# Loads by three units in rows of 24 KB, stores by pairs or units from pair buffers, and two pairs in spent buffers

## Chip, cores, metric

One core of one Trainium2 chip. The metric is the device time of one execution in microseconds (us). Most executions of a kernel agree within a few tenths of a per cent; an execution more than 1.5% above the fastest of the same kernel counts as slow, and comparisons use fast executions only.

## The reference

Attention through 32 inducing points, then a feed-forward network without a residual. B = 4 batches, N = 12480 tokens, C = 128 channels, m = 32, hidden width 2048; everything enters and leaves in fp32.

```python
def mab(q, kv):
    s = scale * (q @ kv.transpose(0, 2, 1))
    s = s - s.max(-1, keepdims=True)
    a = np.exp(s)
    a /= a.sum(-1, keepdims=True) + 1e-09
    return a @ kv
h = mab(I, x)            # 32 inducing points attend to all tokens of a batch
y = mab(x, h)            # every token attends to the 32 rows of h
out = gelu(y @ w_in) @ w_out
```

## The kernel before

A batch is six units of 2048 tokens and a tail of 192. The *first pass* goes over the units of a batch as they are loaded: transposes on the tensor engine (PE), an evacuation into `xT`, scores against the inducing points, exponentials, and a gather into `hun`. When the tail is through, a short *chain* of matmuls makes `h` and `q`, the network applied to the 32 rows (the kernel does that on `h`, not on the tokens). The *second pass* makes scores from `xT`, exponentials, the products with `q`, scales them by the row sums on the vector engine (DVE), the scalar engine (ACT) or ACT and GpSimd (POOL), and stores them. The second pass of a batch runs beside the first pass of later ones.

What the change touches is how tokens are grouped for the DMA. Loads go by *pairs* of units: a partition's row of a pair is 32 tokens, 16 KB of fp32, cast to fp16 on the way, issued by GpSimd. Stores go by pairs from three pair buffers, issued by the sync engine (SP). Pair (b, p) is pair p of batch b. Pair (1, 2) is put into a buffer of `xT` that is no longer needed ("spent"). Batch 3 is stored unit by unit, in 8 KB rows, from six load buffers that have come free.

```python
XBUFS = 6
OBUFS = 3
...
APART = 3
SPENT = (B - 3, 2)
...
        self.pair = idx // 2
        self.c_pair = 0 if self.tail else 16 * (idx % 2)
        self.first = self.c_pair == 0
        self.last = self.tail or not self.first
        self.held = self.nc if self.tail else 32

    def rows_of(self, t):
        t0 = self.b * N + self.pair * 2 * SGT
        t = t[t0 : t0 + self.held * self.p, :]
        return t.rearrange("(p c) d -> p c d", p=self.p)
...
    def x_tile(u):
        if u.tail:
            xh = sb.tile([TP, 2, 128], FP16, tag="xht", bufs=3)
        else:
            xh = sb.tile([128, 32, 128], FP16, tag="xh", bufs=XBUFS)
...
    def a_load(u):
        nc.gpsimd.dma_start(out=x_tile(u), in_=u.rows_of(x_rows))
...
    def b_inverse(bt, u):          # where a unit's output lives
        ...
        elif u.b >= APART:
            o = sb.tile([128, 32, 128], FP16, tag="xh", bufs=XBUFS)
            ...
        else:
            if u.first:
                if spent(u):
                    pair = xt_pool.tile([128, N], FP16, tag="xT", name=f"spent{u.b}")
                    ...
                else:
                    pair = sb.tile([128, 32, 128], FP32, tag="o", bufs=OBUFS)
                bt.live[("pair", u.pair)] = pair
            o = bt.live[("pair", u.pair)][:, u.c_pair : u.c_pair + 16, :]
        bt.live[("o", u.idx)] = o
...
    def b_store(bt, u, alone):     # alone: a tail, or a unit of batch 3
        if alone:
            c0, c1, o = u.c_pair, u.c_pair + u.nc, bt.live[("o", u.idx)]
        else:
            c0, c1, o = 0, u.held, bt.live[("pair", u.pair)]
        nc.sync.dma_start(out=u.rows_of(out)[:, c0:c1, :], in_=o)
```

The order of instructions on each engine is fixed while the kernel is built: a list scheduler runs through all pieces with modelled durations, and a model of the DMA decides when a load or a store is done. That model gives each of the two queues half of the DMA while both have work:

```python
class Moves:
    ...
            steps += [h[1] * len(going) for h in going.values()]
    ...
                    h[1] -= step / len(going)
```

An engine that reaches a piece whose buffer is not yet free waits there, with all the work behind it in the fixed order.

## Time and profile before

| | before |
|---|---|
| device time, median (range) | 133.07 us (132.63 to 133.23, 5 runs) |
| profiled span | 131.5 us |
| DMA engines full | 3 to 128 us |
| compute ends | 121.1 us |
| stores of pair (0, 1) landed | 66.6 us |
| first DVE write into that buffer's next use | 68.22 us |
| first store of batch 3 issued | 108.6 us (one unit) |

### The profile page before, as it was taken

Reading aid. Unit: us, or ns where it says so; the run is one execution under the profiler, and the core shown is the slowest. Engines: PE = TensorE matmul, PEld = TensorE weight load, DVE = VectorE, ACT = ScalarE, POOL = GpSimd, SP = SyncE. Lnnn points to the kernel's source line nnn. Section 1 sums busy time; section 2 is a strip of 40 time slices with the busy share of each in tenths; the row PEclk is TensorE's granted clock in tenths of the full one; section 3 lists DMA queues with packets and bytes.
Section 4 is the critical chain, followed back from the end, with each engine's and each line's share of the span. In section 5 each row is a group of like instructions: output and inputs, shape, how many; then the busy total and the mean of one; then the engine's idle time right before and its main releaser. Section 6 shows DMA issues by size and latency. Waiting matters only on the chain. (4 is left out here: it accounts for less than half of the span.)

```text
span 131.5 us, 3505 instructions
## 1 busy us (share of the span) xinstructions
PE 101.8 (77%) x1365; PEld 60.0 (46%) x1365; DVE 91.9 (70%) x265; ACT 77.1 (59%) x177; POOL 65.6 (50%) x85
## 2 busy tenths in 40 slices
PE   0967789479999999999697699999999499781000
PEld 0255656278646557565362565735645312320000
DVE  1825447525899998999999367999899756997000
ACT  3006154426776879499787378889797457754000
POOL 7910131039634556894815367965269763483000
PEclk9999869855999999999999689999999856999555
DMA  5999999999999999999999999999999999999981
GB/s 152 298 228 209 217 198 219 218 214 222 214 209 214 214 229 339 306 387 368 322 304 339 277 251 297 316 401 411 439 425 415 419 444 419 411 426 424 431 349 43
DMA packets 5666, 40.17 MB, mean 305 GB/s; under 512 B 624, under 2 KB 1936, under 8 KB 2192
## 3 DMA queue, kind: packets, MB, share of 16 engines
q0 software_dynamic: 2848, 13.30, 49.9%
q1 hardware_dynamic: 2752, 26.61, 48.5%
q8 instruction: 11, 0.18, 0.5%
q10 hardware_dynamic: 48, 0.02, 0.1%
q14 instruction: 7, 0.06, 0.1%
HBM read 27.67 MB, written 25.56 MB: 405 GB/s over the span
## 5 line engine op out<-in xcount | busy, mean ns | idle before, releaser
L702 POOL TENSOR_TENSOR pair<-pair,rr 128x512 f32<-128x512 f32 x26 | 26.8, 1043 | 19.6 <-ACT pair L365 16.7
L686 PE MATMUL at<-q,e 128*128 128x512 f16 (+1 forms) x104 | 33.7, 391 | 3.6 <-DVE xT L363 1.2
L377 PE MATMUL tr<-identity_h,xh 128*128 128x128 f16 x392 | 32.7, 244 | 3.1 <-DMA xh<-in_x_dram 3.1
L377 PEld LDWEIGHTS <-xh 128*128 128x128 f16 x392 | 27.5, 111 | 9.2 <-DMA xh<-in_x_dram 4.2
L363 DVE COPY xT<-tr 128x1024 f16<-128x1024 f16 (+1 forms) x36 | 22.7, 646 | 10.1 <-PE tr L377 9.6
L365 ACT ACTIVATE xT<-tr 128x1024 f16<-128x1024 f16 (+1 forms) x16 | 15.7, 980 | 18.6 <-PE tr L377 18.5
L717 DVE TENSOR_TENSOR pair<-at,rr 128x512 f32<-128x512 f32 x36 | 23.3, 676 | 1.1 <-PE at L686 0.4
L287 POOL DMA_DIRECT2D xh<-in_x_dram x15 | 8.3, 555 | 21.3 <-DMA xh<-in_x_dram 10.5
L403 ACT ACTIVATE e<-s 128x512 f16<-128x512 f32 (+1 forms) x28 | 15.3, 546 | 5.7 <-PE s L391 5.4
L638 ACT ACTIVATE e<-s 128x512 f16<-128x512 f32 (+1 forms) x28 | 14.9, 562 | 3.4 <-PE s L626 1.8
L365 ACT ACTIVATE pair<-at 128x512 f32<-128x512 f32 x26 | 15.7, 602 | 1.1 <-PE at L686 1.0
L417 DVE STREAM_TRANSPOSE e1t<-e 128x256 int32<-128x256 int32 (+1 forms) x28 | 11.1, 399 | 3.4 <-ACT e L403 3.3
L686 PEld LDWEIGHTS <-e 128*128 128x128 f16 (+1 forms) x104 | 8.7, 103 | 10.2 <-issue 6.7
L425 PE MATMUL hun<-xh,e1t 128*32 128x128 f16 x392 | 10.8, 226 | 3.1 <-DVE e1t L417 3.0
L572 POOL TENSOR_TENSOR pt<-pt 128x512 f32<-128x512 f32 (+4 forms) x20 | 12.0, 602 | 2.1 <-DVE rr L661 0.7
L717 DVE TENSOR_TENSOR o<-at,rr 128x512 f32<-128x512 f32 (+1 forms) x19 | 10.5, 579 | 2.9 <-PE at L686 2.5
L391 PE MATMUL s<-xT,indT 128*32 128x512 f16 (+1 forms) x108 | 10.5, 379 | 1.4 <-DVE xT L363 0.8
L425 PEld LDWEIGHTS <-e1t 128*32 128x32 f16 x392 | 6.4, 98 | 8.9 <-DVE e1t L417 6.5
L626 PE MATMUL s<-xT,hT 128*32 128x512 f16 (+1 forms) x100 | 10.0, 407 | 0.5 <-DVE rr L661 0.5
L702 POOL TENSOR_TENSOR o<-o,rr 128x512 f32<-128x512 f32 x7 | 7.3, 1041 | 5.7 <-ACT o L365 3.3
L650 PEld LDWEIGHTS <-e 128*128 128x128 f16 (+1 forms) x104 | 5.7, 99 | 4.8 <-issue 1.9
L650 PE MATMUL r<-strand,e 128*128 128x4 f16 (+1 forms) x104 | 6.7, 168 | 0.2 <-ACT e L403 0.2
(76 smaller groups left out, 102.0 us busy)
## 6 DMA issues: line engine op xcount, KB each, us to landing
out_dram<-pair SPq DMA_DIRECT2D x8, 2048.0 KB, 15.0
xh<-in_x_dram POOLq DMA_DIRECT2D x11, 1024.0 KB, 28.2
out_dram<-o SPq DMA_DIRECT2D x6, 1024.0 KB, 8.8
out_dram<-spent SPq DMA_DIRECT2D x1, 2048.0 KB, 16.1
x_first<-in_x_dram SPq DMA_DIRECT2D x1, 1024.0 KB, 5.2
xh<-in_x_dram POOLq DMA_DIRECT2D x1, 512.0 KB, 6.9
w_in_h<-in_moe_w_in_dram POOLq DMA_DIRECT2D x1, 512.0 KB, 17.2
w_out_h<-in_moe_w_out_dram POOLq DMA_DIRECT2D x1, 512.0 KB, 19.2
```

The source lines that it names most:

```text
L363: nc.vector.tensor_copy(out=out, in_=in_)
L365: nc.scalar.activation(out=out, in_=in_, func=AF.Copy)
L377: nc.tensor.transpose(tr[:, c - c0, : u.p], xh[: u.p, c, :], identity_h[: u.p, : u.p])
L403: nc.scalar.activation(out=e1[: u.p, : u.nc // 2, :, :], in_=s1[: u.p, : u.nc, :].rearrange("r (a b) i -> r a i b", b=2), func=AF.Exp, sca ...
L417: nc.vector.transpose(out=pairs(e1t)[: u.p, :n], in_=pairs(e1)[: u.p, :n])
L425: nc.tensor.matmul(bt.hun[32 * j : 32 * j + 32, :], e1t[: u.p, c // 2, :, c % 2], xh[: u.p, c, :], start=u.idx == 0 and c < 4, stop=c + 4 ...
L572: nc.gpsimd.tensor_tensor(out=bt.pt[:, :, :, :half], in0=bt.pt[:, :, :, :half], in1=bt.pt[:, :, :, half : 2 * half], op=ALU.add,)
L638: nc.scalar.activation(out=e2[: u.rows, : u.cols], in_=s2[: u.rows, : u.cols], func=AF.Exp, scale=SCALE,)
L650: nc.tensor.matmul(r2[: u.p, ci, : u.nj], e2[: u.rows, ci * u.p : (ci + 1) * u.p], strand[: u.rows, : u.nj], start=True, stop=True,)
L686: nc.tensor.matmul(at[: u.p, : u.nj, :], e2[: u.rows, ci * u.p : (ci + 1) * u.p], bt.q[: u.rows, : u.nj, :], start=True, stop=True,)
L702: nc.gpsimd.tensor_tensor(out=part, in0=part, in1=rr2[: u.p, ci, : u.nj].unsqueeze(2).broadcast_to([u.p, u.nj, 128]), op=ALU.mult,)
L717: nc.vector.tensor_tensor(out=ov[: u.p, ci, :, :], in0=at[: u.p, : u.nj, :], in1=rr2[: u.p, ci, : u.nj].unsqueeze(2).broadcast_to([u.p, u. ...
```

## The change

The intent: longer rows for loads (24 KB, three units at once, called a *triple* below, so fewer packets and transfers), output by pairs also in batch 3, and no load buffers kept back for outputs. A pair that straddles two triples (pair 1 of each batch) cannot be one row of the new layout, so it is stored as two units in 8 KB rows.

```diff
-XBUFS = 6
+XBUFS = 4
-APART = 3
-SPENT = (B - 3, 2)
+SPENT = ((B - 3, 2), (B - 1, 0))
...
+        self.three = idx // 3
+        self.c_three = 0 if self.tail else 16 * (idx % 3)
+        self.leads = self.c_three == 0
+        self.held = self.nc if self.tail else 48
...
+        self.split = self.pair == 1
...
-        t0 = self.b * N + self.pair * 2 * SGT
+        t0 = self.b * N + self.three * 3 * SGT
...
-            xh = sb.tile([128, 32, 128], FP16, tag="xh", bufs=XBUFS)
+            xh = sb.tile([128, 48, 128], FP16, tag="xh", bufs=XBUFS)
...
-        elif u.b >= APART:
-            o = sb.tile([128, 32, 128], FP16, tag="xh", bufs=XBUFS)
...
+        c1 = u.c_three + u.nc
         if alone:
-            c0, c1, o = u.c_pair, u.c_pair + u.nc, bt.live[("o", u.idx)]
+            c0, o = u.c_three, bt.live[("o", u.idx)]
         else:
-            c0, c1, o = 0, u.held, bt.live[("pair", u.pair)]
+            c0, o = u.c_three - u.nc, bt.live[("pair", u.pair)]
...
-        elif u.first:
+        elif u.leads:
...
-                    move=part(u, LOAD_US) * (1 if u.tail else 2),
+                    move=part(u, LOAD_US) * (1 if u.tail else 3),
...
-        alone = u.tail or u.b >= APART
+        alone = u.tail or u.split
```

More of the change, by code (lines that the diff above doesn't have):

```diff
@@ L96, in __init__ @@
         self.last = self.tail or not self.first
-        self.held = self.nc if self.tail else 32
+        self.split = self.pair == 1
     def rows_of(self, t):
-        t0 = self.b * N + self.pair * 2 * SGT
+        t0 = self.b * N + self.three * 3 * SGT
         t = t[t0 : t0 + self.held * self.p, :]
@@ L106, in spent @@
 def spent(u):
-    return (u.b, u.pair) == SPENT
+    return (u.b, u.pair) in SPENT
 def home_of(u):
@@ L277, in x_tile @@
         else:
-            xh = sb.tile([128, 32, 128], FP16, tag="xh", bufs=XBUFS)
-        x_tiles[(u.b, u.pair)] = xh
+            xh = sb.tile([128, 48, 128], FP16, tag="xh", bufs=XBUFS)
+        x_tiles[(u.b, u.three)] = xh
         return xh
     def x_of(u):
-        xh = x_tiles[(u.b, u.pair)]
-        return xh[:, u.c_pair : u.c_pair + u.nc, :]
+        xh = x_tiles[(u.b, u.three)]
+        return xh[:, u.c_three : u.c_three + u.nc, :]
     def a_load(u):
@@ L292 @@
     x_first = sb.tile([128, 32, 128], FP32, tag="o", bufs=OBUFS)
-    x_pair = x_tile(units[0][0])
+    x_lead = x_tile(units[0][0])
     src = units[0][0].rows_of(x_rows)
     nc.sync.dma_start(out=x_first[:, :16, :], in_=src[:, :16, :])
-    nc.gpsimd.dma_start(out=x_pair[:, 16:, :], in_=src[:, 16:, :])
-    a_load(units[0][2])
+    nc.gpsimd.dma_start(out=x_lead[:, 16:, :], in_=src[:, 16:, :])
+    a_load(units[0][3])
     identity = consts.tile([128, 128], FP32)
@@ L367, in a_cast @@
     def a_cast(c0, engine):
-        evacuate(engine, x_pair[:, c0 : c0 + 8, :], x_first[:, c0 : c0 + 8, :])
+        evacuate(engine, x_lead[:, c0 : c0 + 8, :], x_first[:, c0 : c0 + 8, :])
     def halves(u):
@@ L665, in b_inverse @@
             o = sb.tile([TP, 2, 128], FP32, tag="ot", bufs=2)
-        elif u.b >= APART:
-            o = sb.tile([128, 32, 128], FP16, tag="xh", bufs=XBUFS)
-            o = o.rearrange("p c d -> p (c d)").bitcast(FP32)
-            o = o.rearrange("p (c d) -> p c d", d=128)
         else:
@@ L785, in add_load @@
                 plan.add(
-                    (0, 1), {"POOL": 0.55}, lambda e: None, takes=["xh"], move=LOAD_US
+                    (0, 1), {"POOL": 0.55}, lambda e: None, takes=["xh"], move=2 * LOAD_US
                 )
             )
-        elif u.first:
+        elif u.leads:
             loads.append(
@@ L793, in add_load @@
                     {"POOL": 0.55},
-                    lambda e: None if u.b == 0 and u.idx == 2 else a_load(u),
+                    lambda e: None if u.b == 0 and u.idx == 3 else a_load(u),
                     takes=["xht" if u.tail else "xh"],
-                    move=part(u, LOAD_US) * (1 if u.tail else 2),
+                    move=part(u, LOAD_US) * (1 if u.tail else 3),
                 )
@@ L876 @@
             takes=["hun"] if u.idx == 0 else [],
-            gives=["e1t"] + (["xht"] if u.tail else ["xh"] if u.last else []),
+            gives=["e1t"] + (["xht"] if u.tail else ["xh"] if u.idx % 3 == 2 else []),
         )
@@ L907 @@
         )
-        alone = u.tail or u.b >= APART
-        if alone:
-            o_taken = o_given = ["ot" if u.tail else "xh"]
+        alone = u.tail or u.split
+        if u.tail:
+            o_taken = o_given = ["ot"]
         else:
```

## The prediction

> **What bounds the kernel now.** I read the page's slices first, then the DMA part, the chain that ended last, the DMA issues with their landing times, and the DVE timeline around one store. From the page: the DVE row, the DMA row, the queues, and the last chain by engine.
>
> ```profile
> DVE  1825447525899998999999367999899756997000
> DMA  5999999999999999999999999999999999999981
> ...
> q0 software_dynamic: 2848, 13.30, 49.9%
> q1 hardware_dynamic: 2752, 26.61, 48.5%
> ...
> DVE 3%; PE 1%; issue 1%; ACT 0%
> ```
>
> The 16 DMA engines are full from slice 2 to slice 39 (3 to 128 us): the two queues together take 98% of their time. The compute engines stop at 121 us (last three slices of DVE empty), and the followed chain covers only 5% of the span: what ends at 131.5 us is the stores. So DMA work is the floor. But DVE at 9 tenths from 35 to 70 us and from 80 to 99 us says that compute is the next limit, close behind.
>
> Bytes: 27.67 MB read and 25.56 MB written, 405 GB/s over the span. With loads alone the queue writes 217 GB/s of halves, so reads about 430 GB/s; with stores alone it moves 425 to 430 GB/s. Both are nearly the same rate per byte.
>
> How the two queues share comes from two windows, 51 to 55 us (a load of a pair beside a store of a pair) and 76 to 80 us (the same load beside the 96 KB tail store of batch 0).
>
> ```profile
> q1 hardware_dynamic: 54, 0.88, 52.6%
> q0 software_dynamic: 50, 0.41, 48.8%
> ...
> q0 software_dynamic: 100, 0.69, 82.2%
> q1 hardware_dynamic: 106, 0.40, 26.1%
> ```
>
> Columns: queue, packets, MB, share of the engines' time in the window. In the first, rows are 16 KB on both sides and the packets are 54 to 50: one for one, each 0.62 us (52.6% of 64 us over 54). In the second, the packets are again about one for one, although most store packets there are 1 KB: the loads took 82% of the time. The tail's 6 packets per engine needed 4.0 us (previous store landed at 76.3, tail at 80.3), that is 6 x (0.62 + 0.05). So the queues alternate packet by packet, whatever the size. Packet size is therefore a priority.
>
> **What the Trainium skill says.** "DMA: Bandwidth & Descriptors", section "Queues, rings and completion order": each DMA engine round-robins between queue rows at packet granularity. The two windows agree. Its section "Where 436 GB/s comes from" puts the ceiling at 435 GB/s; the 425 to 430 GB/s here are 98 to 99% of it, so longer rows can win at most 1 to 2%. Its section "Bandwidth" has rates up to 425 GB/s for large loads, as here.
>
> **The change, part by part.**
> *Rows.* Eleven pair loads in 16 KB rows become one such load and seven in 24 KB rows. An 8 KB store row takes 0.31 us and a 16 KB row 0.62 us: no visible fixed cost per row. From 430 against 435 GB/s I estimate under 10 ns per row, so 512 rows fewer save about 512 x 10 ns / 16 = 0.3 us. Splitting one pair per batch into two unit stores, while batch 3 goes from six unit stores to two pairs and two units, adds 128 rows net, less than 0.1 us. Sum: nil, at best 0.3 us faster.
> *Engines.* The order of instructions moves four evacuations of the transposed input from ACT to DVE (4 x 0.65 us more) and four scalings off DVE (4 x 0.65 us less), leaving DVE's sum unchanged near 92 us. PE is unchanged; ACT changes by about 1 us.
> *Start.* Batch 0's units 1 and 2 come together, then 3 to 5. The last lands at 17 us as now, but three units wait for it instead of two. One unit costs PE some 2 us there at half clock, so I put the first store 1.5 to 2 us later, first packet at 49.5 instead of 48.1 us. This is hidden: loads fill the DMA then.
> *Sharing.* With 24 KB load rows (0.92 us, estimate from 0.62) against a pair's 16 KB rows, loads get 60%; against a unit's 8 KB rows, 75%. The split pair is pair 1 of each batch. In batch 0 its stores run just while batch 3's two triples load. Working with 8 rows per engine and transfer: the second triple of batch 2 lands near 56 us; the store of pair (0,0) near 58.6 (now 59.2); a small tail load to 59.5, in which 2.4 rows of the split pair pass; the other 13.6 rows each stand beside a load row: 13.6 x (0.92 + 0.31) = 16.7 us. So both stores of pair (0,1) have landed near 76 us. Now they land at
>
> ```profile
> out_dram<-pair SPq DMA_DIRECT2D x1, 2048.0 KB, 15.5
> ...
> 68.22 1.29 DVE L717 TENSOR_TENSOR pair<-at,rr 128x512 f32<-128x512 f32 x2
> ```
>
> issued 51.05 + 15.5 = 66.6 us. The second line, from DVE's timeline, is the first DVE write into that buffer by pair (1,1): 68.22 us, only 1.6 us after. Three pair buffers stay in the ring, so the changed kernel has the same reuse; its DVE, ACT and GpSimd orders all wait for both (0,1) stores at that place. In exchange batch 3's loads land earlier: about 69 and 79.5 us instead of 73.4 and 89.1.
>
> *What the stall costs.* At that instruction DVE has done 48 of its 95 us in both orders (instruction counts times mean durations of the page's groups). Batch 2's chain and all of batch 3's work stand behind it in DVE's fixed order. DVE would arrive at 69 to 70.5 us and wait until 77: 6 to 8 us. Of this, 2.2 us come back, since DVE now waits that long at 73 to 75 us for a PE that waits for batch 3's load; other waits recover little, because DVE's remaining 46.5 us plus the 4 us of waits around batch 3's chain end at 77 + 50.5 = 127.5. So compute ends at 126 to 128 instead of 121 us.
>
> *From compute to the end.* Now stores run 8 us behind compute, and at 98.5 us the backlog falls to 1.8 units (14 units issued, 12.2 stored), 4.4 us. Delays up to about 4 us are therefore hidden. Beyond, the DMA runs dry. Batch 3's first store is now a unit at 108.6 us; after the change a pair, whose second unit ends now at 111.8 us, so 117 to 118.5 us with the delay. The stores before it (18 units, 3 tails) are through by about 114. Restart at 118.5 to 119.5, then 6 units x 2.45 us = 14.7 us, the tail 0.3 and landing about 1 us: span 134.5 to 135.5, +3 to +4 us, times 136 to 137 from 133.07.
>
> **The rivals.**
> *Nothing changes: the floor holds.* The DMA carries the same bytes and the delay may be smaller than the backlog. For it: the 4.4 us slack, earlier batch 3 loads, a schedule arranged for late loads (batch 2's second pass runs further ahead). Then 132.5 to 133.5. Also so if a 24 KB row goes as two packets: loads then get about 60% against unit rows, the split pair lands near 71 us, and the stall is some 2 us.
> *Loads bound at the start and the larger grain costs.* Three units arriving at once could move all of batch 0 later by 3 us or more. Against it: the DMA is busy with loads up to 48 us anyway, and the next triples have free buffers. Adds 0 to 1 us.
> *Row length lifts the rate.* Against it: 98 to 99% of the ceiling already. Best case 131.5 to 132.5, not a gain of 2% (130.4).
> *Losing batch 3's separate output buffers.* Its six units now have six freed load buffers; after it, a spent buffer and the ring. Pair (3,1) waits for store (2,0), landing now at 104.6, and (3,2) for (2,1), at 109.6; the units need them after 111 us. Adds nothing.
>
> **Range and chances.** I hold the priority theory with its stall at about three in four, centred at 136.3 with 1.3 to either side; it leaves some cases under 2% (135.7). The rest is around 133. Between them: 135.6, range 132.6 to 138.6. Faster by 2% 0.04; within 2% 0.47; slower 0.49.
>
> **What would show it.** Right: in the changed profile, load packets of 0.92 us alternate one for one with store packets while both run; the unit stores of pair (0,1) land near 76 us; DVE, ACT and GpSimd wait at pair (1,1) for a DMA for 6 us or so; DVE ends near 127; the DMA row shows a hole near 110 to 119 us. Wrong: packets not longer than 0.62 us on the load queue; no DVE wait near 70 us; a DMA row full up to 128 us with a time near 133. A time under 131 would contradict the ceiling argument.

## The result, and the profile after

The changed kernel took 141.33 us (median of 5, 140.15 to 143.93; four of them fast) against 133.07 (132.63 to 133.23). The ratio is 1.0617, with a 95% interval of 1.0545 to 1.0689. Every ratio here is the mean time of one kernel's fast runs over the mean of the kernel before's fast runs of the same rounds (in the experiments without the profiled execution), so it is not quite the ratio of the medians quoted. The result is slower, as the prediction leaned, but above its range (132.6 to 138.6).

The page of the changed kernel, slices of 3.5 us and queues:

```profile
DVE  1732568213789898889900569989988745899200
PEclk9995599955699999999997579999999655896555
DMA  6999999999999999999999999999899790399991
...
q0 software_dynamic: 2272, 13.30, 46.7%
q1 hardware_dynamic: 2896, 26.61, 46.4%
```

The bytes are the same (13.30 MB of halves written by loads, 26.61 MB moved by stores and the first load), in 431 packets fewer, and the queues' packets together take 93.1% of 139.4 us, 130 us: the work of the DMA has not grown. What is new is two holes: DVE at 0, 0 and 5 tenths from 70 to 80 us, and the DMA at 0 and 3 tenths from 115 to 122 us. In the kernel before, the DMA row is full from the second slice to the 38th.

The first hole. How the two queues share from 68 to 72 us, where loads of batch 3 meet the unit stores of pair (0, 1) in the changed kernel and a pair store in the one before (queue, packets, MB, share of the engines' time). After:

```profile
q0 software_dynamic: 59, 0.60, 71.0%
q1 hardware_dynamic: 58, 0.48, 29.0%
```

Before:

```profile
q1 hardware_dynamic: 60, 0.98, 58.2%
q0 software_dynamic: 60, 0.39, 46.0%
```

Packets alternate one for one in both. Once the 24 KB rows stand against 8 KB rows (part of this window), loads take nearly three quarters. A 24 KB row takes 926 ns, an 8 KB row 309, a 16 KB row 611 to 625. The second unit store of pair (0, 1), from the list of issues between 52 and 53 us, with its size and the time to landing, then DVE's timeline where that buffer is used next:

```profile
out_dram<-pair SPq DMA_DIRECT2D x1, 1024.0 KB, 25.1
```

```profile
69.78 0.17 DVE L620 TENSOR_REDUCE sums<-pt 128x1 f32<-128x16 f32 x1
77.62 0.69 DVE L718 TENSOR_TENSOR pair<-at,rr 128x512 f32<-128x512 f32 x1 [7.67 <-DMA out_dram<-pair]
```

It was issued at 52.38 us and landed at 77.5, and DVE stood 7.67 us waiting for it. ACT waits 7.7 us for the same store, GpSimd 9.9 us behind ACT.

The second hole. SP's timeline of store issues after, then one stretch of it: window, length, busy us of PE, weight loads, DVE, ACT and POOL (with counts), granted clock (the part of its full clock that PE was given), share of the DMA, GB/s:

```profile
109.26 0.33 SPq L731 DMA_DIRECT2D out_dram<-pair  x1
109.69 0.37 SPq L731 DMA_DIRECT2D out_dram<-o  x1
120.40 0.33 SPq L731 DMA_DIRECT2D out_dram<-spent  x1
122.75 6.58 SPq L731 DMA_DIRECT2D out_dram<-pair  x3
```

```profile
115.50:121.20 5.70, 5.48 (x28) 1.45 (x27) 3.63 (x6) 3.77 (x10) 2.94 (x4) 0.66 0.01 2
```

From 109.7 to 120.4 us no store is issued, and for 5.7 us the DMA moves nothing. The 120.40 is pair (3, 0), the first of batch 3. Everything left, three pairs and a tail, then passes from 121.24 us to the end of the span at 139.4.

From the late write to the end of compute, in three stretches: 20 us, then up to batch 3's `q`, then from there to the last compute instruction. After, then before, both beginning at the first write into that buffer:

```profile
77.60:97.60 20.00, 18.58 (x249) 10.02 (x248) 17.26 (x51) 16.55 (x41) 14.46 (x17) 0.89 1.00 415
97.60:113.40 15.80, 13.99 (x202) 8.47 (x199) 12.31 (x38) 11.63 (x31) 7.67 (x8) 0.87 0.91 375
113.40:130.30 16.90, 12.63 (x62) 3.77 (x59) 13.68 (x41) 10.12 (x28) 9.32 (x12) 0.70 0.64 265
```

```profile
68.20:88.20 20.00, 17.53 (x257) 10.40 (x260) 15.28 (x42) 14.86 (x37) 12.28 (x14) 0.91 1.02 308
88.20:104.70 16.50, 14.71 (x220) 8.39 (x209) 15.06 (x47) 13.19 (x34) 10.61 (x11) 0.98 1.01 425
104.70:121.10 16.40, 12.29 (x68) 3.84 (x65) 13.19 (x43) 9.89 (x25) 8.87 (x11) 0.81 1.00 423
```

The sums are 52.7 and 52.9 us. A write that comes 9.4 us later ends compute 9.2 us later: nothing was made up.

### The profile page after: what moved, and what is told of

Same layout as the page of the kernel before. It is cut to its first block, busy times and chain, and to the rows that moved or that the text cites. A ratio compares the mean times of both kernels' runs of the same rounds, so it can differ in the third digit from the quotient of the medians.

```text
span 139.4 us, 3515 instructions
## 1 busy us (share of the span) xinstructions
PE 103.5 (74%) x1365; PEld 59.8 (43%) x1365; DVE 89.6 (64%) x265; ACT 77.6 (56%) x192; POOL 63.6 (46%) x80
## 3 DMA queue, kind: packets, MB, share of 16 engines
q0 software_dynamic: 2272, 13.30, 46.7%
q1 hardware_dynamic: 2896, 26.61, 46.4%
## 5 line engine op out<-in xcount | busy, mean ns | idle before, releaser
L703 POOL TENSOR_TENSOR pair<-pair,rr 128x512 f32<-128x512 f32 x30 | 31.3, 1049 | 39.6 <-ACT pair L370 32.8
L382 PE MATMUL tr<-identity_h,xh 128*128 128x128 f16 (+1 forms) x392 | 30.9, 238 | 5.6 <-DMA xh<-in_x_dram 5.4
L368 DVE COPY xT<-tr 128x1024 f16<-128x1024 f16 (+1 forms) x41 | 25.6, 642 | 14.7 <-PE tr L382 14.3
L718 DVE TENSOR_TENSOR pair<-at,rr 128x512 f32<-128x512 f32 x40 | 26.3, 675 | 8.6 <-DMA out_dram<-pair 7.7
L382 PEld LDWEIGHTS <-xh 128*128 128x128 f16 (+1 forms) x392 | 26.3, 108 | 11.0 <-DMA xh<-in_x_dram 5.9
L370 ACT ACTIVATE pair<-at 128x512 f32<-128x512 f32 x30 | 18.1, 604 | 9.3 <-DMA out_dram<-pair 7.7
L687 PEld LDWEIGHTS <-e 128*128 128x128 f16 (+1 forms) x104 | 8.9, 103 | 22.5 <-issue 18.8
L370 ACT ACTIVATE xT<-tr 128x1024 f16<-128x1024 f16 x11 | 11.3, 1023 | 11.4 <-PE tr L382 11.4
L711 ACT ACTIVATE pair<-at,rr 128x128 f32<-128x128 f32 x40 | 11.4, 378 | 1.7 <-PE r L655 1.3
L718 DVE TENSOR_TENSOR spent<-at,rr 128x512 f32<-128x512 f32 x9 | 6.0, 688 | 2.6 <-PE at L687 2.5
L703 POOL TENSOR_TENSOR spent<-spent,rr 128x512 f32<-128x512 f32 x6 | 6.4, 1081 | 2.0 <-ACT spent L370 2.0
```

The lines of the kernel that those rows point to most:

```text
L368: nc.vector.tensor_copy(out=out, in_=in_)
L370: nc.scalar.activation(out=out, in_=in_, func=AF.Copy)
L382: nc.tensor.transpose(tr[:, c - c0, : u.p], xh[: u.p, c, :], identity_h[: u.p, : u.p])
L687: nc.tensor.matmul(at[: u.p, : u.nj, :], e2[: u.rows, ci * u.p : (ci + 1) * u.p], bt.q[: u.rows, : u.nj, :], start=True, stop=True,)
L703: nc.gpsimd.tensor_tensor(out=part, in0=part, in1=rr2[: u.p, ci, : u.nj].unsqueeze(2).broadcast_to([u.p, u.nj, 128]), op=ALU.mult,)
L711: nc.scalar.activation(out=ov[: u.p, ci, j, :], in_=at[: u.p, j, :], func=AF.Copy, scale=rr2[: u.p, ci, j : j + 1],)
```

## The experiments

The theory to test: 24 KB load rows hold up the 8 KB store rows of pair (0, 1); the engines wait for that buffer; the wait goes on to batch 3's first store; the DMA runs dry. Rivals: a later start, the output half of the change (bigger grain, no separate buffers), or something in the new order itself. All outputs are right.

### rows8: the first triple of batch 3 in rows of 8 KB

Based on the kernel after; one of its eight bulk loads is split, and nothing moves in the order of compute.

```diff
     def a_load(u):
-        nc.gpsimd.dma_start(out=x_tile(u), in_=u.rows_of(x_rows))
+        xh, src = x_tile(u), u.rows_of(x_rows)
+        step = 16 if (u.b, u.idx) == (B - 1, 0) else u.held
+        for c0 in range(0, u.held, step):
+            nc.gpsimd.dma_start(out=xh[:, c0 : c0 + step, :], in_=src[:, c0 : c0 + step, :])
```

> The changed kernel, with one load, the first triple of batch 3, issued as three transfers in 8 KB rows instead of one in 24 KB rows. Priority theory: beside 0.31 us load rows the 13.6 rows left of pair (0,1) take 13.6 x 0.62 = 8.4 us, so its stores land near 69 us instead of 77.4; the 7.7 us DVE wait falls below 1 us and the time comes back to 133 to 135 us. The triple itself lands later, near 78 us instead of 70. Rival (the three output buffers and the pair stores of batch 3 cost the time, or the coarser loads at the start do): the wait moves but the time stays above 138 us.

Measured: 135.24 us (134.29 to 136.15), 1.0186 [1.0106, 1.0266]. The second unit store landed at 52.76 + 16.6 = 69.4 us, and DVE's first write waited for no store:

```profile
70.23 0.68 DVE L721 TENSOR_TENSOR pair<-at,rr 128x512 f32<-128x512 f32 x1
```

Compute ended at 123.1 us. The load's last part landed at 77.0 us (78 was expected). Rows of one load transfer (1.5 MB as it is written, in halves) carry more than two thirds of the loss.

### rows12: the same triple in two parts of 12 KB rows

The edit is that of rows8 with `step = 24`.

> As the run with 8 KB rows, but the first triple of batch 3 as two transfers in 12 KB rows (0.46 us). Priority theory: 13.6 x (0.46 + 0.31) = 10.5 us, pair (0,1) lands near 71 us, between 69.4 (8 KB) and 77.4 (24 KB); DVE waits about 1 us; the time is 134.5 to 137 us. If only the number of transfers mattered and not the row: like one of the two ends.

Measured: 135.0 us (134.36 to 135.09), 1.0161 [1.0133, 1.0189]; store landed at 52.6 + 18.8 = 71.4 us (71 expected), and DVE waited 1.4 us:

```profile
71.56 0.69 DVE L721 TENSOR_TENSOR pair<-at,rr 128x512 f32<-128x512 f32 x1 [1.40 <-DMA out_dram<-pair]
```

The landing of the store follows the load's row: 8 KB 69.4, 12 KB 71.4, 24 KB 77.5 us. The time does not distinguish the first two.

### before_split: the store half of the cause, in the kernel before

Pair (0, 1) of the kernel before as two transfers of 8 KB rows; loads keep 16 KB rows.

```diff
-        nc.sync.dma_start(out=u.rows_of(out)[:, c0:c1, :], in_=o)
+        step = 16 if (u.b, u.pair) == (0, 1) else c1 - c0
+        for c in range(c0, c1, step):
+            nc.sync.dma_start(
+                out=u.rows_of(out)[:, c : c + step, :], in_=o[:, c - c0 : c - c0 + step, :]
+            )
```

> The kernel before, with only the store of pair (0,1) issued as two transfers in 8 KB rows (loads stay in 16 KB rows). Priority theory: 16 rows of 0.31 us, each beside a load row of 0.62 us (some beside the small tail load), take 5 us longer than 8 rows of 0.62: it lands near 71 us instead of 66.6, the first DVE write of pair (1,1) waits 3 us, and because delays up to 4 us hide behind the store backlog, the time is 133 to 134.5 us. If row size sets no priority: lands near 66.6 us, no wait, 133.1 us.

Measured: 133.59 us (133.35 to 133.82), 1.0048 [1.0008, 1.0087]. The store landed at 52.4 + 20.6 = 73.0 us (71 was expected), 6.4 later than in before, and DVE waited:

```profile
73.16 1.89 DVE L717 TENSOR_TENSOR pair<-at,rr 128x512 f32<-128x512 f32 x3 [3.65 <-DMA out_dram<-pair]
```

A row of half the length on the store side is held up by a 16 KB row too, and a first write 4.9 us later costs only half a per cent: the backlog of stores hides most of it.

### delay4 and delay6: the delay by itself

The kernel before with four or six DVE fills ahead of the first write into that buffer, with the DMA left alone.

```diff
+            if (u.b, u.idx) == (1, 2):
+                for i in range(4):        # delay6: range(6)
+                    nc.vector.memset(o, 0.0)
```

> The kernel before, with four dummy fills (about 2.2 us each, 8.7 us in all) on DVE into the buffer of pair (1,1) ahead of its first write; loads and stores untouched. If a delay of compute at that place explains all of the loss: compute ends near 129.5 us instead of 121, the DMA runs dry for some us after 105 us, and the time is 138 to 141 us. If the changed stores of batch 3 or the triples matter beside the delay: under 137 us.

> The kernel before with six dummy fills instead of four at the first write of pair (1,1). In the run with four, DVE was busy 6.4 us more (98.3 against 91.9), 1.6 us a fill, and not 2.2 as assumed; compute ended 5 us later and the time rose by 4 us. Six fills are 9.6 us, the size by which the changed kernel writes that buffer late (77.6 against 68.2 us). If that delay alone makes the loss: compute ends near 129.5 us and the time is 139 to 141.5 us, like the changed kernel's 141.3. If half of the loss comes from elsewhere: below 138 us.

The first of delay4's fills, from DVE's timeline:

```profile
68.56 1.76 DVE L683 MEMSET pair<- 128x2048 f32 x1 [0.38 <-issue]
```

The next starts at 70.81 us. With the gap a fill is 2.25 us, so the write came 9.0 us late in delay4 and 14.3 in delay6 (the expectation of delay6 left the gaps out). delay4: 137.17 us (135.57 to 137.58), 1.0271 [1.0199, 1.0343], compute end 126.2, only 5.1 us late. delay6: 142.55 us (140.62 to 142.86), 1.0663 [1.059, 1.0737] from two fast runs; its profile, of a slow run, has compute end 131.5, 10.4 late. A delay here does empty the DMA later (dry at 97 to 100 and 105 to 107 us in delay4) and costs per cents. But 9.0 us cost 3.6 us in this order, where 9.4 cost 8.2 after the change. The stretches of delay4, cut like those above:

```profile
77.10:97.10 20.00, 18.65 (x263) 10.77 (x263) 15.87 (x46) 15.86 (x38) 13.30 (x15) 0.85 1.02 367
97.10:112.10 15.00, 13.21 (x179) 7.37 (x178) 13.97 (x42) 11.97 (x32) 9.36 (x9) 1.00 0.75 310
112.10:126.10 14.00, 10.06 (x68) 3.65 (x64) 12.94 (x43) 9.55 (x25) 9.04 (x12) 0.93 1.00 413
```

They sum to 49.0 us, 3.9 less than in before: 1.5 come back ahead of batch 3's `q` (a wait for a load is gone) and 2.4 behind it, where the clock is 0.93 and not 0.81. After the change neither came back. The experiments after_warm and outputs_delay4, below, ask why.

### outputs_only: the output half alone

The kernel before, with pair loads, but batch 3 stored as after the change.

```diff
-APART = 3
-SPENT = (B - 3, 2)
+APART = B
+SPENT = ((B - 3, 2), (B - 1, 0))
```

> The kernel before with only the output half of the change: batch 3 stores by pairs, from a second spent buffer and the ring of three, loads by pairs in 16 KB rows as before. Priority theory: no store row is shorter than a load row, pair (0,1) lands near 66.6 us, batch 3 needs no buffer before it is free, the first store of batch 3 comes 3 us later (pair instead of unit) and the time is 133 to 135 us. Rival (losing batch 3's own output buffers costs the time): 137 us or more, with a wait for a store in batch 3.

Measured: 133.28 us (132.71 to 133.59), 1.0004 [0.9961, 1.0047]. The first store of batch 3 is issued 4 us later than in before, as SP's timeline shows, and still in time:

```profile
112.60 0.33 SPq L729 DMA_DIRECT2D out_dram<-spent  x1
```

Without lateness from elsewhere the output half is free.

### rows8_start: is the start to blame for the rest?

rows8, and batch 0's loads unit by unit.

```diff
-    nc.gpsimd.dma_start(out=x_lead[:, 16:, :], in_=src[:, 16:, :])
-    a_load(units[0][3])
+    for c0 in (16, 32):
+        nc.gpsimd.dma_start(out=x_lead[:, c0 : c0 + 16, :], in_=src[:, c0 : c0 + 16, :])
+    ...                                      # units 3 to 5 in the same way
```

> The kernel of the 8 KB run, and also batch 0's loads unit by unit in 8 KB rows, so that its units land one at a time as early as possible. If what is left of the loss there (135.2 against 133.0) is the later start of compute (first store issued at 46.75 us instead of 44.56): the first store is issued 1.5 us or more earlier and the time is 133 to 134.3. If it is the order and grain later on: 134.8 to 135.6.

Measured: 135.97 us (135.59 to 136.29), 1.025 [1.0223, 1.0277]; the first store went out 1.1 us earlier than in rows8 (45.76 us), and the first write of pair (1, 1) came 1.1 us earlier too (69.11 us, without a wait). But at 89.9 us DVE waited 2.2 us for the store of pair (1, 0), whose buffer pair (2, 1) takes, and compute ended later than in rows8 (125.0 us against 123.2). An earlier start gained nothing here; since another wait stood in its way, this does not rule the start out as a part of the remainder.

### after_unit30 and rows12_unit30: the grain of batch 3's first store

Pair (3, 0) stored as two units, in the kernel after and in rows12. The order of compute is the same.

```diff
-        self.split = self.pair == 1
+        self.split = self.pair == 1 or (b == B - 1 and self.pair == 0)
```

> The changed kernel, with the first pair of batch 3 stored unit by unit from its spent buffer (two transfers in 8 KB rows) instead of as one pair; the order on all compute engines is the same. In the changed kernel the DMA stood empty from 115.7 to 121.2 us, until that pair was issued at 120.4. If the pair's grain makes part of this hole once compute is late: the first unit goes out near 117.3 us, the hole shrinks by some 3 us, and the time falls by 2 to 3 us, to 138 to 139.5. If the hole is the delay alone: within 0.7 us of the changed kernel.

> The 12 KB kernel and the same unit stores for the first pair of batch 3. There the DMA ran low between 112 and 116 us, until that pair was issued at 115.0. If the grain of that store is what keeps it 2 us above the kernel before: first unit issued near 112 us, no hole, 133 to 133.8 us. If something else (clock, order): 134.3 to 135 us.

Measured: after_unit30 139.37 us (139.11 to 140.81), 1.052 [1.0443, 1.0597]; rows12_unit30 133.71 us (133.34 to 134.25), 1.0055 [1.0008, 1.0102]. SP's timeline of after_unit30 has the first store of batch 3 at 118.13 us instead of 120.40:

```profile
118.13 2.99 SPq L731 DMA_DIRECT2D out_dram<-spent  x2
```

The DMA row of after_unit30 first, then that of rows12_unit30 (40 slices of each one's own span):

```profile
DMA  6999999999999999999999999999699878399795
```

```profile
DMA  6999999999998999999999999999999999999980
```

The hole shrinks from 5.5 to 2.4 us in the first (one of 0.9 us comes at 129.3), and there is none in the second. The load's row is worth 6 us (1.0617 to 1.0161). What the grain costs is not settled. In the kernel after it is 1.3 us (1.0617 to 1.052, times 133), with compute ending about as late (130.7 us against 130.3), but the intervals overlap, so that the size rests on the shrunken hole. From rows12 to rows12_unit30 it is 1.4 us (1.0161 to 1.0055) with intervals that do not overlap, but there the clock differed as well: from 74.0 to 80.9 us PE had half clock in the profile of rows12 and the full clock in that of rows12_unit30, and compute ended at 125.4 and 123.4 us. In the latter even the second unit went out at 113.4 us, before the earlier stores had landed (115.3), so a pair would have left no hole there either. Both edits together, with that clock, leave 0.7 us of the 8.2.

### aware_after and aware_before: a scheduler that knows the rows

The scheduler's DMA model shares by row length instead of half and half.

```diff
-            steps += [h[1] * len(going) for h in going.values()]
+            rows = sum(h[2].row for h in going.values())
+            share = {e: h[2].row / rows for e, h in going.items()}
+            steps += [h[1] / share[e] for e, h in going.items()]
```

> The changed kernel with the schedule alone made anew: the planner that fixes each engine's order now shares the DMA by row length between two queues (24 to 8, 24 to 16, 16 to 1) and not half and half. Loads, stores and buffers are as in the changed kernel. If the loss comes from an order that did not know of the late buffer, the engines do other work (batch 2's chain, batch 3's first pass) while pair (0,1) is stored: the wait on that store falls below 2 us and the time is 133 to 136 us. If the late buffer itself is what costs, whatever the order: 138 us or more.

> The kernel before with the schedule made anew by the planner that shares the DMA by row length (it now knows that a tail of 1 KB rows holds a queue for 4 us). If such knowledge helps: 131.5 to 132.8 us. As the DMA is full from 3 to 128 us in the kernel before, I expect no gain over 1%: 132.3 to 133.8 us.

Measured: aware_after 139.33 us (136.98 to 140.77), three of four runs slow, so no interval; DVE still waits 5.0 us and compute ends at 128.1. Its effect on the time stays open; the wait it did not cure. aware_before 132.76 us (132.57 to 133.25), 1.0005 [0.9956, 1.0054]: the kernel before has nothing to win there.

### after_again: the kernel after, unchanged

> The changed kernel once more, on the same chip as the two runs with unit stores: 140 to 142.5 us, with a wait of 7 to 8 us for the store of pair (0,1).

Measured: 142.02 us (139.66 to 143.12), with three of four runs slow, the fast one at 139.66; DVE waited 7.7 us again. The wait repeats; the time adds nothing to the first measurement.

### after_warm: the clock behind batch 3's chain

The granted clock of the kernel after falls to 0.50 just where batch 3's chain runs. Filler matmuls ahead of three of the chain's real ones, for batch 3 alone:

```diff
+        def warm(t, cols, n):
+            if b == B - 1:
+                for _ in range(n):
+                    nc.tensor.matmul(t, blank[:, :128], blank[:, :cols], start=True, stop=True)
...
+            warm(bt.pt_ps.rearrange("p a m -> p (a m)"), 512, 5)     # ahead of up
...
+            warm(bt.qp_ps, 128, 8)                                   # ahead of down
...
+            warm(bt.q_ps, 128, 4)                                    # ahead of the sum of q
```

> The kernel after with filler matmuls ahead of three of the real ones (up, down, sum of q) in batch 3's chain alone, so that the tensor engine does not fall to half clock there. After the change the stretch from batch 3's q to the end of compute took 16.8 us at a granted clock of 0.70; the two kernels with a delay by fills, at 0.94 and 1.0, took 13.9. Theory that the half clock is what kept the delay from coming back: clock above 0.9 in the last 17 us, that stretch about 14 us, compute ends near 127.7 instead of 130.3, time about 139 (1.045 of before). Rival, that the slower matmuls are hidden behind the vector and scalar engines: compute ends at 130 within half a microsecond, time 141 (1.06).

Measured: 139.41 us (138.66 to 139.85), 1.0444 [1.0387, 1.0501], whose interval lies below that of the kernel after. The three stretches from the late write (77.98 us here):

```profile
77.90:97.90 20.00, 19.00 (x239) 10.07 (x238) 16.28 (x49) 15.42 (x39) 13.06 (x15) 0.77 0.98 411
97.90:114.90 17.00, 16.02 (x226) 9.67 (x226) 13.47 (x40) 12.91 (x34) 8.71 (x9) 1.00 0.83 344
114.90:129.50 14.60, 10.48 (x62) 3.88 (x58) 13.54 (x41) 9.91 (x28) 9.44 (x12) 0.83 0.75 306
```

The last is 14.6 us instead of 16.9, as the theory had it. The stretches before it grew from 35.8 to 37.0 us, so compute ended 0.8 us earlier (129.5) and not 2.6. The fillers need not be the reason for that: PE was at half clock here from 73.4 to 87.1 us, around and behind the stall, against 75.1 to 81.9 us in the kernel after, and the unchanged kernel did the same in after_again (72.9 to 86.5 us, and 37.1 us up to `q`; a slow run). The half clock in the chain is one part of what the delay could have won back: 2.3 us in that stretch.

### outputs_delay4: the output half under a late compute

outputs_only with delay4's fills: late compute, pair loads, the order of before.

> The kernel before with the output half of the change and the four fills, 9.0 us on the vector engine: the same delay as in delay4 (1.0271 of before), pair loads and no triple anywhere. Theory that the rest of what the changed kernel lost lies in its output half once compute is late: compute ends near 126 as in delay4, but the first store of batch 3 waits for two units and goes out near 117 instead of at the first unit's end, so a hole in the DMA of some 2 to 4 us and about 138.5 to 139 (1.04 to 1.045). Rival, that it lies in the order that goes with the triple loads: 137 as delay4 (1.03). If compute itself ends near 130 and the time is 141, then the output half alone keeps the delay from coming back.

Measured: 137.69 us (137.28 to 141.13; one slow), 1.0307 [1.0245, 1.0369]. The stretches sum to 49.0 us as in delay4, and compute ends at 126.4. The first store of batch 3 went out at 117.03 us and left no hole of some microseconds. So neither what this theory said of a hole nor the third possibility holds: the output half does not keep the delay from coming back. What is left is the order of instructions that goes with the triple loads, with the clock that it gets. The counterpart is in rows8, which has the order of the kernel after and no wait for a store. Its stretches from its first write:

```profile
70.20:90.20 20.00, 18.59 (x279) 10.22 (x268) 17.52 (x55) 16.52 (x42) 14.63 (x17) 1.00 1.02 324
90.20:106.00 15.80, 13.72 (x197) 8.34 (x197) 12.06 (x37) 11.69 (x31) 7.63 (x7) 0.89 1.01 425
106.00:123.10 17.10, 12.96 (x64) 3.93 (x61) 13.71 (x41) 10.13 (x28) 9.36 (x12) 0.70 0.97 406
```

52.9 us, against 52.7 with the stall: this order takes that long from there whether it is late or not. The other fast profiles in this order lie around it: 52.1 us in rows12_unit30, 52.8 in after_unit30, 53.9 in rows12. Which instructions of the order cost the time is not shown.

## Why the prediction was right or wrong

**The floor and the rate: right.** The DMA's work did not shrink with longer rows (129 to 130 us of packets in both kernels: 98.4% of 131.5 and 93.1% of 139.4). Of the engines' work, five evacuations and five scalings changed hands, where four and four were said; DVE's sum went from 91.9 to 89.6 us. No version beat the kernel before; the best variants only come back to it.

**Sharing: right, in mechanism and size.** A 24 KB row took 926 ns (0.92 said), the stores of pair (0, 1) landed at 77.5 us (76), batch 3's triples at 70.1 and 80.4 us (69 and 79.5). Three lengths of load row beside the same stores move the landing as the alternation says (69.4 and 71.4 us, where 69 and 71 were expected); the split in the kernel before moves it the same way, but 2 us further than expected. The rival of two packets per row is out.

**The start: the size right.** The first packet of a store passed at 49.4 us (49.5 said, 48.1 before); it was issued at 46.0 us instead of 44.6. The DMA was full with loads there, as said. rows8_start won nothing by an earlier start, but met another wait.

**The wait: right.** DVE waited 7.7 us (6 to 8 said), its first write came at 77.62 us (77).

**What the stall costs: here it failed.** The step said "Of this, 2.2 us come back", from DVE's wait for a PE that waits for batch 3's load. That wait was read in the profile of before, where it is real: before's waits of DVE from 68.2 to 121.1 us (total, times, longest) list it second.

```profile
DVE o L717 <- PE at L686: 2.5, 5, 0.8
DVE xT L363 <- PE tr L377: 2.2, 1, 2.2
```

The same group in the kernel after, from 77.6 to 130.3 us, and in rows8, from 70.2 to 123.1 us:

```profile
DVE xT L368 <- PE tr L382: 0.6, 1, 0.6
```

```profile
DVE xT L371 <- PE tr L385: 0.9, 2, 0.6
```

But the change gave the engines another order, and there the wait does not exist to be given back: the same group has 0.6 us in the kernel after, and rows8, without any stall, takes 52.9 us from the same place to the end. Other waits stand in its place: without the stall, the waits that DVE's list shows behind that write add up to 8.1 us in the kernel after and to 8.0 in before. Where that wait was left in the order, as in delay4, it did come back. Compute ended at 130.3 us, where 77 + 50.5 = 127.5 was said: 0.6 of the 2.8 is the later write, 2.2 the recovery. The two terms of the 50.5 were both off: behind the write DVE had 43.3 us of work and not 46.5, and 9.4 us without work and not 4 (43.5 and 9.4 in before). The working also counted DVE alone, while up to `q` PE is the busier engine by the profile's count (32.6 of 35.8 us, DVE 29.6).

A second thing could have come back and did not: the kernel before ends with a stretch that is partly at half clock (0.81 in the mean), which a delay happened to remove (16.4 us to 14.0 in delay4); the order after the change keeps it (16.9). The prediction had not looked at the clock there. after_warm shows its weight in that stretch, 2.3 us. The stall has a half clock of its own, from 75.1 to 81.9 us. What such windows can cost is seen in rows12 and rows12_unit30, with the same order and the same load rows and their first writes at 71.6 and 71.4 us: 36.5 us up to `q` with two of them, 34.9 us with none. The Trainium skill, "TensorE: Matmul & The Clock Gate", Part 1, says that a clock gate halves the clock in windows of 3413 ns by how busy PE has been. The trace agrees in the grid: three windows of 3.4 us at 0.50, from 109.2 to 119.4 us.

**From compute to the end: the mechanism right, both sizes too small.** Stores ran dry as said, and the first of batch 3 ended the hole. It was issued at 120.40 us and not at 117 to 118.5, which is the term above passed on. Then the drain: 16.0 us were said from the restart to the end of the span (14.7 + 0.3 + 1), 18.2 were measured. The six units took 15.7, to the end of their last packet at 136.9 us, and what was left of the tail, with its landing, 2.5 instead of 1.3. In the window from 136 us to the end, the changed kernel's DMA shows the tail's rows of 1 KB beside small instruction fetches:

```profile
DMA packets 132, 0.14 MB, mean 41 GB/s; under 512 B 32, under 2 KB 128, under 8 KB 128
```

**The sum.** Restart 119 + 16.0 = 135 us of span was the middle of the working; it became 121.2 + 18.2 = 139.4. Half of the 4.4 us is the restart, half the drain. On top of that the number on record mixed the working's 136.3 with a quarter's weight on "nothing changes", which did not come true.

**The rival on batch 3's buffers: "Adds nothing" was half right.** Alone it costs nothing (outputs_only). Once compute is late, storing the first pair of batch 3 by units shortened the hole of the kernel after (5.5 to 2.4 us); what that is worth in time is not settled (1.3 us, with intervals that overlap). In the order of before (outputs_delay4 against delay4) no cost can be told from the intervals.

**The 4 us said to be hidden: right.** before_split's write came 4.9 us late and cost 0.6 us.

What stays open: the last 0.7 us between rows12_unit30 and before; the share of the grain of batch 3's first store, apart from the clock; what sets how long the half clock behind the stall lasts (6.8 us in the kernel after, 13.7 in after_again); and whether a scheduler that knows row lengths would help the kernel after, since its runs were slow.

## What to carry to other kernels

Before lengthening rows on one DMA queue, see which rows on the other queue share its time, and which buffer waits for those: a longer row on one side is a lower priority for the other, and it can be paid back by splitting a single transfer (here one load, 1.5 MB as written, worth 6 us). A wait that a delay should absorb has to be looked for in the order that the change makes, not in the old profile. And when a store is the first after the queue has run dry, its grain can show (the hole fell from 5.5 to 2.4 us in after_unit30); while there was a backlog, it showed nothing (outputs_only).

## What the Trainium skill lacked or had wrong

- "DMA: Bandwidth & Descriptors", "Queues, rings and completion order", says that an engine alternates between queues by packet. It does not say what follows for row lengths: in these traces a packet record is one row and the rows of the two queues pass one for one, so the queue with the longer rows gets the larger share (71% in the window above). Here a pair's output landed at 77.5 us instead of 66.6, and rows of 8, 12 and 24 KB on the load side gave 69.4, 71.4 and 77.5.
- The same page, "Bandwidth", advises batching transfers to at least 1 MiB. It does not speak of what a batch does to another queue: here one load of 1.5 MB (as written, in rows of 24 KB as read) made the kernel slower by 4.6% of its time than the same bytes in two parts of 0.75 MB.
- "TensorE: Matmul & The Clock Gate", Part 1, gives half clock after at least one idle window and full clock after one busy window. In the kernel after, the three windows at 0.50 followed a window with PE busy, as the profile counts it, for 2.55 of 3.40 us and no pause over 0.9 us, and they were busy for 2.95, 2.81 and 3.40 us themselves. Only after the last of these did the full clock come back. In rows12, PE was busy for all of 74.0 to 80.9 us, two windows at half clock, so there one such window was not enough. These are the four windows, with PE's busy time as the first figure after the length:

```profile
105.80:109.20 3.40, 2.55 (x45) 1.77 (x45) 3.13 (x11) 2.18 (x9) 2.17 (x3) 1.00 0.81 333
109.20:112.60 3.40, 2.95 (x49) 1.55 (x48) 1.82 (x12) 2.50 (x6) 1.72 (x3) 0.50 0.80 337
112.60:116.00 3.40, 2.81 (x18) 1.29 (x18) 2.12 (x6) 0.60 (x1) 3.01 (x6) 0.50 0.80 313
116.00:119.40 3.40, 3.40 (x16) 0.60 (x17) 1.67 (x3) 2.23 (x6) 1.92 (x2) 0.50 0.00 0
```
